# Two of four token chunks transposed by DMA ahead of use, rstd of the first tiles by Sqrt, and the last tile in halves

## The chip, the cores and the metric

The kernel runs on one core of a Trainium2 chip. A core has five engines with their own instruction queues, which run beside each other and wait for each other through semaphores: TensorE (PE in the profile, with PEld for its weight loads), VectorE (DVE), ScalarE (ACT), GpSimd (POOL) and SyncE (SP), which here only issues DMAs. The metric is the device time of one execution in microseconds, and what counts is the median over several executions.

## What is computed

x has 2048 tokens of 512 features, in bf16. The reference normalizes x and gives the result to two branches: an attention over a sliding window of 8 keys, 2 tokens apart, with 32 heads of 16 features, and a gated feed-forward block with 1792 hidden features. The output is x plus the product of the attention and the Silu of the feed-forward block.

```python
def _layernorm(x, axis=-1, eps=1e-5):
    m = jnp.mean(x, axis=axis, keepdims=True)
    v = jnp.var(x, axis=axis, keepdims=True)
    return (x - m) / jnp.sqrt(v + eps)
...
    def _A_ref(x, wqkv, wo):
        ...
        logits = jnp.einsum("bhsd,bhswd->bhsw", q, kg) * scale
        logits = jnp.where(mask[None, None, :, :], logits, -1e9)
        attn = _softmax(logits, axis=-1)
        o = jnp.einsum("bhsw,bhswd->bhsd", attn, vg)
        return (lambda x, *d: x.transpose(*d))(o, 0, 2, 1, 3).reshape(B, S, D) @ wo
    def _B_ref(x, w_gate, w_up, w_down):
        g = jnp.einsum("bsd,df->bsf", x, w_gate)
        u = jnp.einsum("bsd,df->bsf", x, w_up)
        h = _gelu(g) * u
        return jnp.einsum("bsf,fd->bsd", h, w_down)
    x = A_x
    xn = _layernorm(x, axis=-1)
    s = _A_ref(xn, A_wqkv, A_wo)
    g = _silu(_B_ref(xn, B_w_gate, B_w_up, B_w_down))
    return x + s * g
```

## The kernel before

The 2048 tokens are 16 tiles of 128 (t) and four chunks of 512 (j), four tiles each. For each chunk there are three stages, in which PE works nearly without a pause: qkv (12 groups of four matmuls that give q, k and v with features on the partitions), glu (14 groups: gate and up products, Gelu on ACT, their product h on DVE), and down (four tiles: the 14 matmuls of the down product y, the four of the attention's output product s, then Silu, product and sum). The order of stages is qkv of chunk 0, glu of chunk 0, qkv of chunk 1, down of chunk 0, glu of chunk 1, qkv of chunk 2, down of chunk 1, and so on: a chunk's qkv stage stands between the glu and the down stage of the chunk before.

Each engine runs its instructions in the order in which the program's text issues them; there is no scheduler. What belongs to another chunk is put between by a table: `at((stage, j, i), fn, ...)` hangs a step ahead of group i of a stage, and `run(stage, j, i)` issues what hangs there (lines 392 to 438 hold the table, 467 to the end the loops).

The steps that the change touches:

- `moments(t)` (line 169) takes mean and variance of a tile on DVE, adds epsilon on DVE, and takes the power -0.5 on GpSimd to get rstd. `normalize(t)` (line 179) makes xn on DVE, one of four buffers of the pool sm4.
- `transpose(t)` (line 186) makes four 128x128 transposes of xn on PE into one PSUM tile `tr`, which ACT copies into `xnT[j]` (features on partitions, the moving operand of all qkv and glu matmuls). xnT has two buffers, so chunk 2 takes chunk 0's and chunk 3 takes chunk 1's.
- The table puts chunk 1's transposes into the glu stage of chunk 0, and those of chunks 2 and 3 into the qkv stages of chunks 1 and 2:

```python
        at(("qkv", 1, 1 + 3 * i), transpose, 2 * TPQ + i)
        at(("qkv", 2, 3 + 2 * i), transpose, 3 * TPQ + i)
```

- `warm_up(n, cols)` (line 200) issues matmuls on zeros, so that PE isn't idle until the first data is there.
- `project` (line 208) is the group of four matmuls, one for each block of 128 input features. `qkv(j, fo, i0, n)` (line 220) is a group with its evacuation by ACT; for chunk 0 it runs over two halves of 256 tokens.
- `down(j, tt)` (line 357) treats the very last tile in two column halves from s onwards, with the second half's store issued by ACT; y and its Silu are whole.
- All PSUM tiles of `tr`, `qkv_ps`, `g_ps`, `u_ps`, `y_ps`, `s_ps`, `sp_ps` and the warm-up rotate through five buffers (pool mm).
- SyncE's queue holds, in this order: the loads of x and the weights; then for each chunk the stores of v to a DRAM scratch (`vT<-vst`, line 235, in the qkv stage), and in the down stage by turns a load of shifted v (`v_arr<-vT`, line 243) and a store of the output (line 387).

Of the kernel before, what the change touches and what calls it, by code (L numbers as in the profile page):

```python
# [9 lines left out]
AF = mybir.ActivationFunctionType  # L10
BF16 = mybir.dt.bfloat16
F32 = mybir.dt.float32

P = 128
# [7 lines left out]
TQ = 512  # L22
VW = TQ + WL * DIL
EPS = 1e-5
# [4 lines left out]
def kernel(  # L29
# [13 lines left out]
    nc = tc.nc  # L43
    B, S, D = A_x.shape
    DF = B_w_gate.shape[1]
    NT, NC, NF, NJ = S // P, D // P, DF // P, S // TQ
    TPQ = TQ // P
    SV = PAD + S
    x2d, out2d = A_x[0], out[0]
# [3 lines left out]
    def pool(name, bufs, **kw):  # L53
        return ctx.enter_context(tc.tile_pool(name=name, bufs=bufs, **kw))

    const = pool("const", 1)
# [7 lines left out]
    xtp = pool("xtp", 2)  # L64
# [5 lines left out]
    mm = pool("mm", 5, space=bass.MemoryType.PSUM)  # L70
# [3 lines left out]
    x_sb = big.tile([P, NT, D], BF16, name="x_sb")  # L74
    wqkv_sb = wts.tile([P, NC, 3 * D], BF16, name="wqkv_sb")
    wg_sb = wts.tile([P, NC, DF], BF16, name="wg_sb")
    wu_sb = wts.tile([P, NC, DF], BF16, name="wu_sb")
    wd_sb = wts.tile([P, NF, D], BF16, name="wd_sb")
# [24 lines left out]
    def load_late_weights():  # L103
# [7 lines left out]
            )  # L111


    warm = const.tile([P, TQ], BF16, name="warm")
    nc.vector.memset(warm[:], 0.0)
    ident = const.tile([P, P], BF16, name="ident")
    make_identity(nc, ident[:])
# [1 line left out]
        out=vT.rearrange("(k p) n -> p k n", p=P)[:, :, 0:PAD],  # L119
        in_=warm[:, 0 : NC * PAD].rearrange("p (k n) -> p k n", k=NC),  # L120
# [19 lines left out]
    def sum_constants():  # L140

        nc.gpsimd.memset(dsum[:], 0.0)
        for c in range(NC):
            nc.gpsimd.memset(dsum[:, c, 8 * c : 8 * c + 8], 1.0)
            band(dsum[:, c, 8 * c : 8 * c + 8], 0, 16, 16, 1, 8)
        for j in range(WL):
            nc.gpsimd.tensor_copy(
                out=hsum[H * j : H * (j + 1), :],
                in_=ident[H * j : H * (j + 1), H * j : H * (j + 1)],
            )  # L150
        nc.gpsimd.memset(spread[:], 0.0)
        for q in range(4):
            for j in range(4):
                nc.gpsimd.tensor_copy(
                    out=spread[H * q : H * (q + 1), q, H * j : H * (j + 1)],
                    in_=ident[H * q : H * (q + 1), H * q : H * (q + 1)],
                )

    xnT = {}
    k_sb = big.tile([P, NC, PAD + S], BF16, name="k_sb")  # L160
    nc.vector.memset(k_sb[:, :, 0:PAD], 0.0)
    stats = const.tile([P, NT, nc.vector.BN_STATS_DIM], F32, name="stats")
    mv = const.tile([P, NT, nc.vector.BN_AGGR_DIM], F32, name="mv")
    mhalf = const.tile([P, 1], F32, name="mhalf")
    nc.gpsimd.memset(mhalf[:], -0.5)
    rstd = const.tile([P, NT, 1], F32, name="rstd")


    def moments(t):
        nc.vector.bn_stats(out=stats[:, t, :], in_=x_sb[:, t, :])  # L170
        nc.vector.bn_aggr(out=mv[:, t, :], in_=stats[:, t, :])
        nc.vector.tensor_scalar(  # L172
            out=rstd[:, t, :], in0=mv[:, t, 1:2], scalar1=EPS, scalar2=None, op0=ALU.add
        )
        nc.gpsimd.tensor_tensor(out=rstd[:, t, :], in0=rstd[:, t, :], in1=mhalf[:], op=ALU.pow)  # L175

    xns = {}

    def normalize(t):
        xn = xns[t] = sm4.tile([P, D], BF16, name="xn")  # L180
        nc.vector.tensor_scalar(
            out=xn[:], in0=x_sb[:, t, :], scalar1=mv[:, t, 0:1], scalar2=rstd[:, t, :],
            op0=ALU.subtract, op1=ALU.mult,
        )

    def transpose(t):
        xn = xns[t]
        tr = mm.tile([P, NC * P], BF16, name="tr", tag="mm")
        for c in range(NC):
            nc.tensor.transpose(tr[:, c * P : (c + 1) * P], xn[:, c * P : (c + 1) * P], ident[:])  # L190
        j, i = divmod(t, TPQ)
        if i == 0:
            xnT[j] = xtp.tile([P, NC, TQ], BF16, name="xnT")
        nc.scalar.activation(  # L194
            out=xnT[j][:, :, i * P : (i + 1) * P],
            in_=tr[:].rearrange("p (c n) -> p c n", c=NC),
            func=AF.Copy,
        )

    def warm_up(n, cols):  # L200

        ps = mm.tile([P, TQ], F32, name="warm_ps", tag="mm")
        for _ in range(n):
            nc.tensor.matmul(
                ps[:, 0:cols], lhsT=warm[:, 0:P], rhs=warm[:, 0:cols], start=True, stop=True
            )

    def project(ps, w, lo, j, i0=0, n=TQ):
        for dk in range(NC):
            nc.tensor.matmul(  # L210
                ps[:],
                lhsT=w[:, dk, lo : lo + P],
                rhs=xnT[j][:, dk, i0 : i0 + n],
                start=(dk == 0),
                stop=(dk == NC - 1),
            )

    st = [dict(pk={}, pv={}) for _ in range(NJ)]

    def qkv(j, fo, i0=0, n=TQ):  # L220
        which, c = divmod(fo, NC)
        if fo == 0 and i0 == 0:
            st[j]["q"] = qp.tile([P, NC, TQ], BF16, name="q_sb")
        ps = mm.tile([P, n], F32, name="qkv_ps", tag="mm")
        project(ps, wqkv_sb, fo * P, j, i0, n)
        if which == 0:
            nc.scalar.activation(out=st[j]["q"][:, c, i0 : i0 + n], in_=ps[:], func=AF.Copy)  # L227
        elif which == 1:
            lo = PAD + j * TQ + i0
            nc.scalar.activation(out=k_sb[:, c, lo : lo + n], in_=ps[:], func=AF.Copy)  # L230
        else:
            vst = sm4.tile([P, TQ], BF16, name="vst")
            nc.scalar.activation(out=vst[:], in_=ps[:], func=AF.Copy)  # L233
            lo = PAD + j * TQ
            nc.sync.dma_start(out=vT[c * P : (c + 1) * P, lo : lo + TQ], in_=vst[:])
# [119 lines left out]
        st[j][fc] = h  # L355

    def down(j, tt):
        y = mm.tile([P, D], F32, name="y_ps", tag="mm")
        for fc in range(NF):
            nc.tensor.matmul(  # L360
                y[:],
                lhsT=st[j][fc][:, tt * P : (tt + 1) * P],
                rhs=wd_sb[:, fc, :],
                start=(fc == 0),
                stop=(fc == NF - 1),
            )
        sl = sm2.tile([P, D], BF16, name="sl")
        nc.scalar.activation(out=sl[:], in_=y[:], func=AF.Silu)  # L368
        t = j * TPQ + tt
        o_t = sm4.tile([P, D], BF16, name="o_t")  # L370
        pieces = 2 if t == NT - 1 else 1
        n = D // pieces
        for i in range(pieces):
            cols = slice(i * n, (i + 1) * n)
            s = mm.tile([P, n], F32, name="s_ps", tag="mm")
            for g in range(NC):
                nc.tensor.matmul(  # L377
                    s[:],
                    lhsT=st[j]["oT"][:, g, tt * P : (tt + 1) * P],
                    rhs=wo_sb[:, g, cols],  # L380
                    start=(g == 0),
                    stop=(g == NC - 1),
                )
            m = sm2.tile([P, n], BF16, name="m")
            nc.vector.tensor_tensor(out=m[:], in0=s[:], in1=sl[:, cols], op=ALU.mult)  # L385
            nc.vector.tensor_tensor(out=o_t[:, cols], in0=m[:], in1=x_sb[:, t, cols], op=ALU.add)
            (nc.scalar if i else nc.sync).dma_start(
                out=out2d[t * P : (t + 1) * P, cols], in_=o_t[:, cols]
            )


    side = {}
# [1 line left out]
    def at(key, fn, *args):  # L394
        side.setdefault(key, []).append((fn, args))
# [5 lines left out]
    for i in range(TPQ):  # L401
        at(("qkv", 0, i), normalize, TPQ + i)
        at(("glu", 0, 7 + i), moments, 2 * TPQ + i)
        at(("glu", 0, i), transpose, TPQ + i)
        at(("glu", 0, 8 + i), normalize, 2 * TPQ + i)
        at(("qkv", 1, 1 + 3 * i), transpose, 2 * TPQ + i)
        at(("glu", 1, 10 + i), moments, 3 * TPQ + i)
        at(("qkv", 2, 2 * i), normalize, 3 * TPQ + i)
        at(("qkv", 2, 3 + 2 * i), transpose, 3 * TPQ + i)

    for w in range(W):
        at(("glu", 0, w), qk_product, 0, w)
# [26 lines left out]


    HT = TPQ // 2
    warm_up(9, TQ)
    moments(0)
    moments(1)
    normalize(0)
    transpose(0)
    normalize(1)
    warm_up(2, P)
    transpose(1)
    warm_up(2, P)  # L450
    moments(2)
    moments(3)
    normalize(2)
    normalize(3)
    for t in range(TPQ, 2 * TPQ):
        moments(t)
    sum_constants()
    for hh in range(2):
        for fo in range(2 * NC):
            qkv(0, fo, hh * HT * P, HT * P)  # L460
            if hh == 0 and fo in (2, 4):
                transpose(HT + fo // 2 - 1)
    for i in range(NC):
        run("qkv", 0, i)
        run("qkv", 0, NC + i)
        qkv(0, 2 * NC + i)
# [41 lines left out]
```

The softmax here doesn't subtract the row's maximum and nothing guards it: scores larger than these inputs give would overflow.

## Time and profile before

| What | us |
|---|---|
| median of 8 runs | 234.62 |
| lowest and highest run | 234.46 and 234.8 |
| the profiled execution, its time | 234.71 |
| the profiled execution, its span | 233.0 |

The span is what the profiler shows of the program, from its first to its last instruction; 1.7 us of the execution's time lie around it. Where the time goes, by stage (PE busy in the stretch, and the engines' own stages don't overlap on PE):

| Stretch of the span, us | What runs on PE | Length | PE busy |
|---|---|---|---|
| 0 to 7.5 | warm-up, two tiles transposed | 7.51 | 5.10 |
| 7.5 to 18.6 | qkv of chunk 0 | 11.09 | 11.04 |
| 18.6 to 46.0 | glu of chunk 0, chunk 1 transposed | 27.40 | 27.24 |
| 46.0 to 59.2 | qkv of chunk 1, chunk 2 transposed, attention of chunk 0 | 13.20 | 13.10 |
| 59.2 to 74.8 | down of chunk 0 | 15.60 | 15.55 |
| 74.8 to 103.4 | glu of chunk 1, attention of chunk 1 | 28.60 | 28.28 |
| 103.4 to 114.7 | qkv of chunk 2, chunk 3 transposed | 11.30 | 11.25 |
| 159.0 to 169.4 | qkv of chunk 3 | 10.40 | 10.35 |
| 213.6 to 233.0 | down of chunk 3 and the end | 19.40 | 15.50 |

A line of a timeline reads: start in us, length in us, engine, line of the program, operation, what it writes and what it reads, shapes, how many in a row; in brackets the idle time of the engine ahead of it and what ended it. SPq is SyncE's queue issuing a DMA. Consecutive matmuls overlap in the records, so what one costs PE is the distance between starts.

### The profile page before, as it was taken

To read this page: it belongs to the slowest core of one execution; us is meant where nothing else is said; L and a number is where in the kernel's file an instruction comes from. 1 tells how busy PE (TensorE), PEld (TensorE's weight loads), DVE (VectorE), ACT (ScalarE), POOL (GpSimd) and SP (SyncE) were. 2 spreads that over 40 slices of the span, in tenths; PEclk is the share of its full clock that TensorE was granted. 3 is DMA by queue.
4 is the path that set the end of the run, shared out by engine and by line. 5 is a ranking of instruction groups with operands and counts; after the bars stand their busy time and mean duration, and the time that the engine had idled before them with its cause. 6 is when DMAs were issued, how large, how long until landed. Compare 5 with 4: busy or idle time off the path is not lost.

```text
span 233.0 us, 3499 instructions
## 1 busy us (share of the span) xinstructions
PE 225.2 (97%) x1321; PEld 105.5 (45%) x1345; DVE 146.4 (63%) x232; ACT 135.6 (58%) x222; POOL 24.5 (11%) x64
## 2 busy tenths in 40 slices
PE   7899999999999999999999999999999999999993
PEld 2775444444444444445444444444444444444441
DVE  4583996996795198981669139951349429864132
ACT  2779869777513865758821396657641387576211
POOL 3248943100000000130000000000000000000000
PEclk9999999999999999999999999999999999999999
DMA  5999399921288200000257600000047910000001
GB/s 156 362 373 366 102 203 203 286 81 48 70 184 200 50 0 0 3 0 0 82 140 177 153 1 3 0 0 3 23 126 169 199 32 0 0 3 1 23 23 45
DMA packets 21937, 22.66 MB, mean 97 GB/s; under 512 B 1568, under 2 KB 21920, under 8 KB 21920
## 3 DMA queue, kind: packets, MB, share of 16 engines
q1 hardware_dynamic: 21776, 22.37, 36.3%
q8 instruction: 10, 0.16, 0.3%
q10 hardware_dynamic: 144, 0.07, 0.1%
q14 instruction: 7, 0.06, 0.1%
HBM read 18.22 MB, written 4.21 MB: 96 GB/s over the span
## 4 chain that ended last, share of the span: by engine, by line
PE 93%; DMA 2%; ACT 1%; issue 1%; SPq 1%; DVE 1%; ACTq 0%
PE u_ps L210 21%; PE y_ps L360 21%; PE g_ps L210 20%; PE qkv_ps L210 18%; PE s_ps L377 6%; PE o_ps L325 3%; PE L_ps L265 3%; DMA wqkv_sb<-in_A_wqkv_dram 2%; PE tr L190 1%; ACT u L352 1%; SPq L83 1%; PE den_ps L285 0%; PE sp_ps L300 0%; DVE m L385 0%; ACT sl L368 0%
## 5 line engine op out<-in xcount | busy, mean ns | idle before, releaser
L210 PE MATMUL u_ps<-xnT,wu_sb 128*128 128x512 bf16 x221 | 57.0, 379 | 0.2
L210 PE MATMUL g_ps<-xnT,wg_sb 128*128 128x512 bf16 x212 | 55.9, 379 | 0.8 <-issue 0.5
L360 PE MATMUL y_ps<-wd_sb,h 128*128 128x512 bf16 x220 | 50.6, 379 | 0.2
L255 DVE TENSOR_TENSOR pk<-q_sb,k_sb 128x2048 bf16<-128x2048 bf16 x32 | 37.8, 1219 | 12.2 <-ACT k_sb L230 12.2
L354 DVE TENSOR_TENSOR h<-ge,u 128x512 bf16<-128x512 bf16 x56 | 23.7, 424 | 34.1 <-ACT u L352 33.9
L210 PE MATMUL qkv_ps<-xnT,wqkv_sb 128*128 128x512 bf16 (+1 forms) x219 | 43.9, 348 | 1.0 <-DMA wqkv_sb<-in_A_wqkv_dram 0.8
L350 ACT ACTIVATE ge<-g_ps 128x512 bf16<-128x512 f32 x56 | 33.6, 601 | 14.4 <-PE g_ps L210 12.3
L352 ACT ACTIVATE u<-u_ps 128x512 bf16<-128x512 f32 x56 | 33.6, 600 | 13.9 <-PE u_ps L210 13.9
L311 DVE TENSOR_TENSOR pv<-E,v_arr 128x2048 bf16<-128x2048 bf16 x32 | 38.6, 1216 | 0.0
L368 ACT ACTIVATE sl<-y_ps 128x512 bf16<-128x512 f32 x16 | 9.6, 597 | 43.9 <-PE y_ps L360 40.6
L210 PEld LDWEIGHTS <-wu_sb 128*128 128x128 bf16 x224 | 21.9, 98 | 26.6 <-issue 0.3
L360 PEld LDWEIGHTS <-h 128*128 128x128 bf16 x224 | 21.9, 98 | 26.4
L210 PEld LDWEIGHTS <-wg_sb 128*128 128x128 bf16 x224 | 20.8, 98 | 26.7 <-issue 4.2
L210 PEld LDWEIGHTS <-wqkv_sb 128*128 128x128 bf16 x224 | 21.3, 98 | 18.6 <-DMA wqkv_sb<-in_A_wqkv_dram 1.0
L385 DVE TENSOR_TENSOR m<-s_ps,sl 128x512 bf16<-128x512 f32 (+1 forms) x17 | 11.2, 656 | 26.8 <-PE s_ps L377 24.4
L175 POOL TENSOR_TENSOR rstd<-rstd,mhalf 128x1 f32<-128x1 f32 x16 | 10.4, 653 | 78.1 <-DVE rstd L172 78.1
L377 PE MATMUL s_ps<-wo_sb,oT 128*128 128x512 bf16 (+1 forms) x68 | 16.4, 367 | 0.1
L170 DVE BATCH_NORM_STATS2 stats<-x_sb 128x6 f32<-128x512 bf16 x16 | 11.0, 686 | 4.3 <-DMA x_sb<-in_A_x_dram 4.3
L227 ACT ACTIVATE q_sb<-qkv_ps 128x512 bf16<-128x512 f32 (+1 forms) x20 | 10.2, 512 | 4.9 <-PE qkv_ps L210 4.6
L233 ACT ACTIVATE vst<-qkv_ps 128x512 bf16<-128x512 f32 x16 | 9.6, 597 | 5.0 <-PE qkv_ps L210 5.0
L194 ACT ACTIVATE xnT<-tr 128x512 bf16<-128x512 bf16 x16 | 9.5, 597 | 4.0 <-PE tr L190 4.0
L230 ACT ACTIVATE k_sb<-qkv_ps 128x512 bf16<-128x512 f32 (+1 forms) x20 | 10.2, 512 | 2.1 <-PE qkv_ps L210 1.9
(42 smaller groups left out, 121.5 us busy)
## 6 DMA issues: line engine op xcount, KB each, us to landing
v_arr<-vT SPq DMA_DIRECT2D x16, 520.0 KB, 5.1
vT<-vst SPq DMA_DIRECT2D x16, 128.0 KB, 1.7
out_dram<-o_t SPq DMA_DIRECT2D x15, 128.0 KB, 2.6
wg_sb<-in_B_w_gate_dram SPq DMA_DIRECT2D x2, 896.0 KB
wu_sb<-in_B_w_up_dram SPq DMA_DIRECT2D x2, 896.0 KB, 13.2
wd_sb<-in_B_w_down_dram SPq DMA_DIRECT2D x1, 1792.0 KB, 17.2
wqkv_sb<-in_A_wqkv_dram SPq DMA_DIRECT2D x3, 512.0 KB, 5.8
x_sb<-in_A_x_dram SPq DMA_DIRECT2D x3, 512.0 KB, 10.1
```

Of the source, the lines that this page charges most:

```text
L170: nc.vector.bn_stats(out=stats[:, t, :], in_=x_sb[:, t, :])
L175: nc.gpsimd.tensor_tensor(out=rstd[:, t, :], in0=rstd[:, t, :], in1=mhalf[:], op=ALU.pow)
L210: nc.tensor.matmul(ps[:], lhsT=w[:, dk, lo : lo + P], rhs=xnT[j][:, dk, i0 : i0 + n], start=(dk == 0), stop=(dk == NC - 1),)
L227: nc.scalar.activation(out=st[j]["q"][:, c, i0 : i0 + n], in_=ps[:], func=AF.Copy)
L255: nc.vector.tensor_tensor(out=pk[:], in0=st[j]["q"][:], in1=k_sb[:, :, off : off + TQ], op=ALU.mult)
L311: nc.vector.tensor_tensor(out=pv[:], in0=st[j]["E"][:, wh, :].unsqueeze(1).to_broadcast([P, 4, TQ]), in1=st[j]["va"][:, 4 * g : 4 * g + 4, ...
L350: nc.scalar.activation(out=ge[:], in_=g_ps[:], func=AF.Gelu_apprx_tanh)
L352: nc.scalar.activation(out=u[:], in_=u_ps[:], func=AF.Copy)
L354: nc.vector.tensor_tensor(out=h[:], in0=ge[:], in1=u[:], op=ALU.mult)
L360: nc.tensor.matmul(y[:], lhsT=st[j][fc][:, tt * P : (tt + 1) * P], rhs=wd_sb[:, fc, :], start=(fc == 0), stop=(fc == NF - 1),)
L377: nc.tensor.matmul(s[:], lhsT=st[j]["oT"][:, g, tt * P : (tt + 1) * P], rhs=wo_sb[:, g, cols], start=(g == 0), stop=(g == NC - 1),)
L385: nc.vector.tensor_tensor(out=m[:], in0=s[:], in1=sl[:, cols], op=ALU.mult)
```

## The change

Six things, in the order of the program's text:

1. The warm-up tile has 256 columns instead of 512, with 17 matmuls of 256 columns instead of 9 of 512, and runs of four instead of two small ones between the first transposes.
2. For the first four tiles rstd is computed as the reciprocal (DVE) of Sqrt(variance + epsilon) (ACT). A Sqrt over a constant at the start brings that function's table in ahead of the data. The other twelve tiles keep the power on GpSimd.
3. Chunk 0's first half of tokens: the four q groups are multiplied feature block pair by feature block pair (blocks 0 and 1 of all four, then 2 and 3), tile 1's copy is in two pieces, and the tiles 2 and 3 are transposed after the q groups, with their copies on DVE. The moments of chunk 1 come after that.
4. The tiles of chunks 2 and 3 are transposed by DMA: 16 requests of 128x128 for a chunk, on SyncE's queue, issued at the head of the glu stages of chunks 1 and 2. Their PE transposes and ACT copies are gone.
5. `project` and `qkv` get arguments for item 3.
6. In `down` the last tile's y and Silu are also made in two halves, each followed by its own s, product, sum and store, both stores on SyncE.

```diff
--- before.py
+++ after.py
@@ -111,7 +111,7 @@
             )
 
 
-    warm = const.tile([P, TQ], BF16, name="warm")
+    warm = const.tile([P, TQ // 2], BF16, name="warm")
     nc.vector.memset(warm[:], 0.0)
     ident = const.tile([P, P], BF16, name="ident")
     make_identity(nc, ident[:])
@@ -166,6 +166,23 @@
     rstd = const.tile([P, NT, 1], F32, name="rstd")
 
 
+    epsc = const.tile([P, 1], F32, name="epsc")
+    nc.gpsimd.memset(epsc[:], EPS)
+    std = const.tile([P, TPQ, 1], F32, name="std")
+
+    nc.scalar.activation(out=std[:, 0, :], in_=epsc[:], func=AF.Sqrt, bias=epsc[:], scale=1.0)
+
+    def first_moments(t):
+        nc.vector.bn_stats(out=stats[:, t, :], in_=x_sb[:, t, :])
+        nc.vector.bn_aggr(out=mv[:, t, :], in_=stats[:, t, :])
+        nc.scalar.activation(
+            out=std[:, t, :], in_=mv[:, t, 1:2], func=AF.Sqrt, bias=epsc[:], scale=1.0
+        )
+
+    def first_normalize(t):
+        nc.vector.reciprocal(out=rstd[:, t, :], in_=std[:, t, :])
+        normalize(t)
+
     def moments(t):
         nc.vector.bn_stats(out=stats[:, t, :], in_=x_sb[:, t, :])
         nc.vector.bn_aggr(out=mv[:, t, :], in_=stats[:, t, :])
@@ -183,7 +200,7 @@
             op0=ALU.subtract, op1=ALU.mult,
         )
 
-    def transpose(t):
+    def transpose(t, parts=1, copy=None):
         xn = xns[t]
         tr = mm.tile([P, NC * P], BF16, name="tr", tag="mm")
         for c in range(NC):
@@ -191,11 +208,14 @@
         j, i = divmod(t, TPQ)
         if i == 0:
             xnT[j] = xtp.tile([P, NC, TQ], BF16, name="xnT")
-        nc.scalar.activation(
-            out=xnT[j][:, :, i * P : (i + 1) * P],
-            in_=tr[:].rearrange("p (c n) -> p c n", c=NC),
-            func=AF.Copy,
-        )
+        dst = xnT[j][:, :, i * P : (i + 1) * P]
+        src = tr[:].rearrange("p (c n) -> p c n", c=NC)
+        for k in range(parts):
+            c = slice(k * NC // parts, (k + 1) * NC // parts)
+            if copy is None:
+                nc.scalar.activation(out=dst[:, c], in_=src[:, c], func=AF.Copy)
+            else:
+                copy(out=dst[:, c], in_=src[:, c])
 
     def warm_up(n, cols):
 
@@ -205,8 +225,19 @@
                 ps[:, 0:cols], lhsT=warm[:, 0:P], rhs=warm[:, 0:cols], start=True, stop=True
             )
 
-    def project(ps, w, lo, j, i0=0, n=TQ):
-        for dk in range(NC):
+    def transpose_by_dma(t):
+        j, i = divmod(t, TPQ)
+        if i == 0:
+            xnT[j] = xtp.tile([P, NC, TQ], BF16, name="xnT")
+        for c in range(NC):
+            nc.sync.dma_start(
+                out=xnT[j][:, c, i * P : (i + 1) * P],
+                in_=xns[t][:, c * P : (c + 1) * P],
+                transpose=True,
+            )
+
+    def project(ps, w, lo, j, i0=0, n=TQ, dks=range(NC)):
+        for dk in dks:
             nc.tensor.matmul(
                 ps[:],
                 lhsT=w[:, dk, lo : lo + P],
@@ -217,12 +248,13 @@
 
     st = [dict(pk={}, pv={}) for _ in range(NJ)]
 
-    def qkv(j, fo, i0=0, n=TQ):
+    def qkv(j, fo, i0=0, n=TQ, ps=None):
         which, c = divmod(fo, NC)
         if fo == 0 and i0 == 0:
             st[j]["q"] = qp.tile([P, NC, TQ], BF16, name="q_sb")
-        ps = mm.tile([P, n], F32, name="qkv_ps", tag="mm")
-        project(ps, wqkv_sb, fo * P, j, i0, n)
+        if ps is None:
+            ps = mm.tile([P, n], F32, name="qkv_ps", tag="mm")
+            project(ps, wqkv_sb, fo * P, j, i0, n)
         if which == 0:
             nc.scalar.activation(out=st[j]["q"][:, c, i0 : i0 + n], in_=ps[:], func=AF.Copy)
         elif which == 1:
@@ -355,23 +387,22 @@
         st[j][fc] = h
 
     def down(j, tt):
-        y = mm.tile([P, D], F32, name="y_ps", tag="mm")
-        for fc in range(NF):
-            nc.tensor.matmul(
-                y[:],
-                lhsT=st[j][fc][:, tt * P : (tt + 1) * P],
-                rhs=wd_sb[:, fc, :],
-                start=(fc == 0),
-                stop=(fc == NF - 1),
-            )
+        t = j * TPQ + tt
+        halves = [slice(0, D // 2), slice(D // 2, D)] if t == NT - 1 else [slice(0, D)]
+        n = D // len(halves)
         sl = sm2.tile([P, D], BF16, name="sl")
-        nc.scalar.activation(out=sl[:], in_=y[:], func=AF.Silu)
-        t = j * TPQ + tt
         o_t = sm4.tile([P, D], BF16, name="o_t")
-        pieces = 2 if t == NT - 1 else 1
-        n = D // pieces
-        for i in range(pieces):
-            cols = slice(i * n, (i + 1) * n)
+        for i, cols in enumerate(halves):
+            y = mm.tile([P, n], F32, name="y_ps", tag="mm")
+            for fc in range(NF):
+                nc.tensor.matmul(
+                    y[:],
+                    lhsT=st[j][fc][:, tt * P : (tt + 1) * P],
+                    rhs=wd_sb[:, fc, cols],
+                    start=(fc == 0),
+                    stop=(fc == NF - 1),
+                )
+            nc.scalar.activation(out=sl[:, cols], in_=y[:], func=AF.Silu)
             s = mm.tile([P, n], F32, name="s_ps", tag="mm")
             for g in range(NC):
                 nc.tensor.matmul(
@@ -384,9 +415,7 @@
             m = sm2.tile([P, n], BF16, name="m")
             nc.vector.tensor_tensor(out=m[:], in0=s[:], in1=sl[:, cols], op=ALU.mult)
             nc.vector.tensor_tensor(out=o_t[:, cols], in0=m[:], in1=x_sb[:, t, cols], op=ALU.add)
-            (nc.scalar if i else nc.sync).dma_start(
-                out=out2d[t * P : (t + 1) * P, cols], in_=o_t[:, cols]
-            )
+            nc.sync.dma_start(out=out2d[t * P : (t + 1) * P, cols], in_=o_t[:, cols])
 
 
     side = {}
@@ -403,10 +432,10 @@
         at(("glu", 0, 7 + i), moments, 2 * TPQ + i)
         at(("glu", 0, i), transpose, TPQ + i)
         at(("glu", 0, 8 + i), normalize, 2 * TPQ + i)
-        at(("qkv", 1, 1 + 3 * i), transpose, 2 * TPQ + i)
+        at(("glu", 1, 0), transpose_by_dma, 2 * TPQ + i)
         at(("glu", 1, 10 + i), moments, 3 * TPQ + i)
         at(("qkv", 2, 2 * i), normalize, 3 * TPQ + i)
-        at(("qkv", 2, 3 + 2 * i), transpose, 3 * TPQ + i)
+        at(("glu", 2, 0), transpose_by_dma, 3 * TPQ + i)
 
     for w in range(W):
         at(("glu", 0, w), qk_product, 0, w)
@@ -439,27 +468,37 @@
 
 
     HT = TPQ // 2
-    warm_up(9, TQ)
-    moments(0)
-    moments(1)
-    normalize(0)
+    HQ = HT * P
+    warm_up(17, TQ // 2)
+    first_moments(0)
+    first_moments(1)
+    first_normalize(0)
     transpose(0)
-    normalize(1)
-    warm_up(2, P)
-    transpose(1)
-    warm_up(2, P)
-    moments(2)
-    moments(3)
-    normalize(2)
-    normalize(3)
+    first_normalize(1)
+    warm_up(4, P)
+    transpose(1, parts=2)
+    warm_up(4, P)
+    first_moments(2)
+    first_moments(3)
+    first_normalize(2)
+    first_normalize(3)
+
+    qs = [mm.tile([P, HQ], F32, name="qkv_ps", tag="mm") for _ in range(NC)]
+    for dks in ((0, 1), (2, 3)):
+        for fo in range(NC):
+            project(qs[fo], wqkv_sb, fo * P, 0, 0, HQ, dks)
+    for fo in range(NC):
+        qkv(0, fo, 0, HQ, qs[fo])
+    transpose(HT, copy=nc.vector.tensor_copy)
+    for fo in range(NC, 2 * NC):
+        qkv(0, fo, 0, HQ)
+        if fo == NC:
+            transpose(HT + 1, copy=nc.vector.tensor_copy)
     for t in range(TPQ, 2 * TPQ):
         moments(t)
     sum_constants()
-    for hh in range(2):
-        for fo in range(2 * NC):
-            qkv(0, fo, hh * HT * P, HT * P)
-            if hh == 0 and fo in (2, 4):
-                transpose(HT + fo // 2 - 1)
+    for fo in range(2 * NC):
+        qkv(0, fo, HQ, HQ)
     for i in range(NC):
         run("qkv", 0, i)
         run("qkv", 0, NC + i)
```

## Prediction

> **What bounds the kernel now.** I read the page's busy shares first, then the chain of work that ended last, then the timeline of the tensor engine where the change touches it, and SyncE's own timeline, because the change gives SyncE new work.
>
> ```profile
> PE 225.2 (97%) x1321; PEld 105.5 (45%) x1345; DVE 146.4 (63%) x232; ACT 135.6 (58%) x222; POOL 24.5 (11%) x64
> PE 93%; DMA 2%; ACT 1%; issue 1%; SPq 1%; DVE 1%; ACTq 0%
> ```
>
> PE is busy for 97% of the span and carries 93% of the chain. So an edit pays only where it takes work off PE, or where PE stands still now: the start, and the last microseconds. The start, from the chain in order of time:
>
> ```profile
> 2.66 4.81 DMA wqkv_sb<-in_A_wqkv_dram
> 7.46 0.05 issue
> 7.51 1.48 PE qkv_ps L210 x12
> ```
>
> The first real matmul waits for the first third of wqkv, landed at 7.46. The stage table by windows has PE busy 11.04 of the 11.09 us from there to the first glu stage: no hole to win. One qkv stage, from the PE timeline (start, us, instruction, count):
>
> ```profile
> 103.34 2.75 PE L210 MATMUL qkv_ps<-xnT,wqkv_sb 128*128 128x512 bf16 x12
> 105.93 0.39 PE L190 MATMUL tr<-ident,xn 128*128 128x128 bf16 x4
> 106.15 1.89 PE L210 MATMUL qkv_ps<-xnT,wqkv_sb 128*128 128x512 bf16 x8
> ```
>
> The busy time of matmuls overlaps, so the price of a tile's transpose is from start to start: 106.15 - 105.93 = 0.22 us, not the 0.39 shown. SyncE's timeline between the store that ends a down stage and the first store of the next qkv stage:
>
> ```profile
> 76.16 0.33 SPq L387 DMA_DIRECT2D out_dram<-o_t  x1
> 112.60 3.13 SPq L235 DMA_DIRECT2D vT<-vst  x4
> ...
> 131.58 0.33 SPq L387 DMA_DIRECT2D out_dram<-o_t  x1
> 167.51 2.91 SPq L235 DMA_DIRECT2D vT<-vst  x4
> ```
>
> SyncE issues nothing in the glu stages of chunks 1 and 2, and the stage table has the DMA engines 8% busy there. The end, from the timeline of all engines:
>
> ```profile
> 228.12 1.04 PE L377 MATMUL s_ps<-wo_sb,oT 128*128 128x256 bf16 x8
> 228.32 0.60 ACT L368 ACTIVATE sl<-y_ps 128x512 bf16<-128x512 f32 x1 [3.29 <-PE y_ps L360]
> 228.95 0.42 DVE L385 TENSOR_TENSOR m<-s_ps,sl 128x256 bf16<-128x256 f32 x1 [2.43 <-ACT sl L368]
> 229.41 0.29 DVE L386 TENSOR_TENSOR o_t<-m,x_sb 128x256 bf16<-128x256 bf16 x1
> 229.62 0.42 DVE L385 TENSOR_TENSOR m<-s_ps,sl 128x256 bf16<-128x256 f32 x1
> ```
>
> Both halves of the last tile wait for one Silu over 512 columns, then go through DVE one after the other.
>
> **What the Trainium skill says.** "VectorE: DVE Perf Modes", section on the three transpose paths, puts a 128x128 bf16 transpose at 390 ns on TensorE and 1309 ns through the DMA crossbar. The trace has 0.22 us of PE time for four in a pipeline, so the first figure is a lone latency; no run here shows the second. "DMA: Bandwidth & Descriptors", in its rules for kernel authors, says that a transpose next to ordinary DMAs needs nothing; untested here. "ScalarE: Activation LUTs", section on what ACT_TABLE_LOAD costs, gives 1283 ns whatever the set; the trace's loads are all 1283 ns. "TensorE: Matmul & The Clock Gate", part 1, says that the array runs at half clock until it was busy for a window of about 3.4 us that doesn't start with the kernel. The trace agrees in kind: warm-up matmuls of 512 columns start 0.43 us apart, later ones 0.22.
>
> **The change part by part.**
>
> Transposes of chunks 2 and 3. Removed: 8 tiles of 4 PE transposes, 8 x 0.22 = 1.76 us, all on the path, since PE is without a hole in both qkv stages; and 8 ACT evacuations of 0.6 us, beside PE. Not all of it comes through. In chunk 1's qkv stage the spread matmuls (sp_ps, line 300) wait for the reciprocals:
>
> ```profile
> 50.06 0.95 DVE L294 RECIPROCAL rs<-den_ps 128x128 bf16<-128x128 f32 x1
> ```
>
> That ends at 51.01, behind a DVE queue with no gap since 43.66, so it doesn't move. sp_ps starts at 51.38 now; two removed tiles (at 46.28 and 50.29) bring it to 50.94, where it must wait until about 51.07 (0.06 us from DVE's end to PE, as at the first transpose, 5.30 to 5.36). I deduct 0.13. What else is near doesn't bite: the last attention product ends at 54.35 and its sums move from 56.46 to about 55.7; in chunk 2's qkv stage DVE idles 5.80 us before its products.
>
> Added: 16 DMA transposes of 128x128 for each of the two chunks, in SyncE's queue behind the store above. The order of the built program has nothing else between that store and the v stores of the next stage, so they start at 76.16 + 0.33 = 76.5 and 131.9. Each has a semaphore of eight in rotation, so it waits for the one eight places earlier. PE wants the first rows of the new xnT at 103.34 and the sixteenth piece (last column block) three matmuls of 0.22 later, 104.0; for chunk 3, 159.08 + 0.65 = 159.7. Stages ahead of it shorten both sides alike. The cost c of one is unseen. From below: 0.33 us, what the store of 128 rows takes to issue. From above: no overlap at all, issue plus landing of a v store, 0.33 + 1.7 = 2.03 us (the page's median to landing is 1.7). I take the skill's 1.309: 16 x 1.309 = 20.9, plus 1.7 for the last to land, 76.5 + 22.6 = 99.1, and 154.5. That is 4.9 and 5.2 us ahead of need. So PE never waits: cost nothing, hidden by the glu stage. It stays so up to c = (104.0 - 76.5 - 1.7) / 16 = 1.61 us. Queued behind a late one would be the next stage's v stores, not due before 112.6.
>
> What reads and frees buffers: the normalize of chunk 3 (in chunk 2's qkv stage) overwrites xn after the DMAs read it, which PE needed first anyway. The two xnT buffers were last read by the glu stage before. Nothing new waits there.
>
> rstd by Sqrt, splitting, order of the start. An Add and a Power on GpSimd (0.55 us and a hop) give way to a Sqrt on ACT and a reciprocal of one column on DVE. The Sqrt isn't in the trace; near 0.3 us, below the 0.38 of a 256-column ACTIVATE; the reciprocal near the 0.15 of the one-column Add. Tile 0's xn starts at about 4.95 (4.89 before), since DVE does tile 1's moments first; tile 1's goes from 5.75 to about 5.5. Both are done well before 7.46, when the weights land, and those are requested in the same place: gain 0. The table load is one for one, at 0.80, under the loads of x. Behind 7.51 PE does the same multiplications and two transposes in another order. The third transpose now comes at 7.51 + 16 x 0.109 = 9.25, and its xn is there at 8.5 even by the old path; the two copies moved to DVE (0.6 us each) end near 10.9, and the second half of the columns starts at 11.4. So 0 again, with bounds of -0.2 and +0.3, five PSUM buffers in rotation being the reason for the upper one.
>
> The end. The last tile's down product in two halves: 28 matmuls of 0.109 for 14 of 0.216, the same 3.0 us. Half 0's Silu, product and store run under half 1's matmuls. Then y of half 1 ends its issue at 225.10 + 1.52 + 0.44 + 1.53 = 228.59; Silu 0.2 later, 0.38 long, to 229.17; s ends at 229.03, and 0.27 later (as for the tile before) DVE may start: 229.30. Product 0.42 and addition 0.29 with their small gaps end at 230.04, against 230.35 now. The last store is issued by SyncE and not by ACT, 0.33 for 0.38. Gain 0.31; bounds 0.1 to 0.45.
>
> Sum: 1.76 - 0.13 + 0 + 0.31 = 1.94 us. The profiled execution took 234.71 (span 233.0 and 1.7 around it), so 232.8 for its like; it lies 0.09 above the median of 234.62, so 232.7 for a median. Own range of this case 232.0 to 233.4.
>
> **The rivals.**
>
> Transposes late (slower). One mechanism: SyncE or the crossbar takes more than 1.61 us for each, and PE stands at the head of the qkv stages of chunks 2 and 3. With the upper price, 2.03, the last lands at 76.5 + 32.5 = 109.0 and 164.4: 5.0 + 4.7 = 9.7 us late, less 1.94: 234.62 + 7.8 = 242.4. For it: the trace shows no such DMA, they are small, 32 KB, and there are 16 of them in one queue. Against it: 4.9 us to spare at the page's figure, an empty queue and idle DMA engines.
>
> Half the gain. Removing transposes brings PE up against DVE and PSUM evacuation at more places than sp_ps, for instance the attention sums in chunk 1's qkv stage, and chunk 1's 0.9 us is lost: 233.6. For it: DVE is busy 11.13 of 13.2 us in that stage. Against: each later dependence has 0.7 us or more in hand.
>
> Cold start. The warm-up now has 17 x 256 columns for 9 x 512, ends 0.25 us earlier, and PE idles longer before the first xn. If the clock is still halved at 7.51, up to 3.4 us run at half speed: 1.7 us lost, total 234.4, no change. Against: the two runs of extra small warm-up matmuls, and 3.6 us of unbroken work.
>
> **How the numbers follow.** Forecast 0.66, half the gain 0.06, cold start 0.04, late 0.24. A change below 0.2% (0.47 us) can't be told from none here. Faster: forecast and half the gain, less a rest, 0.71. Same: 0.05. Slower: 0.24. The three cases other than late lie between 232.0 and 234.5 and hold 0.76, so the range must take in the milder half of late: up to 242.5. It is 232.0 to 242.5.
>
> **What would show it.** Right: no tr in the two qkv stages; those stages 0.75 and 0.9 us shorter; PE's qkv_ps not waiting for a DMA of xnT; the last transpose landed before 104 less what came earlier; the last o_t about 0.3 us closer to the last y_ps; the first qkv_ps still near 7.5, released by wqkv_sb. Wrong: DMA xnT as what PE waits for, at 1.6 us or more for each request; matmuls 0.2 us apart at 256 columns after 7.5; a new idle row before s_ps or o_ps.

## Result and profile after

The changed kernel takes 232.72 us in the median of 11 runs (232.41 to 233.23), against 234.61 for the kernel before in the same comparison. The ratio is 0.9916, 95% interval 0.9906 to 0.9925: faster by 0.84%. Of the kernel before, 1 execution of 32 here took 236.28 us, and 3 or 4 of 27 beside each later group of runs took 236.15 to 236.79 at a mean granted clock of 0.989 to 0.993, which widens the intervals and hardly moves the medians. The profiled execution took 232.77 with a span of 231.1, against 234.71 and 233.0. The page of the changed kernel begins as follows, with the busy shares and further down the chain by engine:

```profile
PE 223.6 (97%) x1315; PEld 106.5 (46%) x1339; DVE 147.0 (64%) x234; ACT 132.2 (57%) x219; POOL 22.1 (10%) x61
...
PE 91%; DVE 4%; ACT 2%; DMA 1%; issue 1%; ACTq 0%; DVEq 0%
```

PE lost 1.6 us of busy time and still fills 97% of the span. But DVE's share of the chain went from 1% to 4%: somewhere the kernel now waits for DVE. SyncE's timeline of the changed kernel, at the ends of the down stages of chunks 0 and 1:

```profile
75.47 0.33 SPq L418 DMA_DIRECT2D out_dram<-o_t  x1
75.91 21.89 SPq L233 DMA_TRANSPOSE xnT<-xn  x16
...
130.00 0.33 SPq L418 DMA_DIRECT2D out_dram<-o_t  x1
130.43 20.73 SPq L233 DMA_TRANSPOSE xnT<-xn  x16
```

16 requests take 21.9 and 20.7 us, 1.37 and 1.30 each. The trace gives 2.3 us in the median from a request to its landing, so the last of chunk 2, requested near 75.91 + 21.89 - 1.23 = 96.6, lands near 98.9. PE wants it near 103.3. The next stage of the kernel before, then this stretch of the changed one:

```profile
114.59 1.67 PE L360 MATMUL y_ps<-wd_sb,h 128*128 128x512 bf16 x7
```

```profile
101.78 1.03 PE L241 MATMUL u_ps<-xnT,wu_sb 128*128 128x512 bf16 x4
102.65 10.52 PE L241 MATMUL qkv_ps<-xnT,wqkv_sb 128*128 128x512 bf16 x47
113.01 3.18 PE L398 MATMUL y_ps<-wd_sb,h 128*128 128x512 bf16 x14
```

The stage runs from 102.65 to 113.01 in one piece, 10.36 us against 11.25 (103.34 to 114.59), and no line of PE's waits names xnT. Chunk 1's qkv stage shows where DVE comes in; PE's timeline before, then after:

```profile
48.45 1.04 PE L325 MATMUL o_ps<-pv,hsum 128*32 128x512 bf16 x16
```

```profile
47.98 0.82 PE L357 MATMUL o_ps<-pv,hsum 128*32 128x512 bf16 x12
49.07 0.40 PE L357 MATMUL o_ps<-pv,hsum 128*32 128x512 bf16 x4 [0.27 <-DVE pv L343]
49.40 1.90 PE L241 MATMUL qkv_ps<-xnT,wqkv_sb 128*128 128x512 bf16 x7
51.14 0.39 PE L332 MATMUL sp_ps<-rs,spread 128*128 128x128 bf16 x4
```

The first attention sums, which ran in one piece before (48.45 to 49.42), now stop after 12 of 16 matmuls, until DVE has the fourth product pv. The view names 0.27 us of idle time; from the first sum to the next qkv matmul it is 1.42 us instead of 0.97. PE begins the stage 0.25 us earlier, but DVE's products stand where they stood. DVE's timeline before, then after:

```profile
42.99 0.41 DVE L181 TENSOR_SCALAR xn<-x_sb,mv,rstd 128x512 bf16<-128x512 bf16 x1 [0.44 <-POOL rstd L175]
46.65 3.49 DVE L311 TENSOR_TENSOR pv<-E,v_arr 128x2048 bf16<-128x2048 bf16 x3
```

```profile
43.06 0.41 DVE L198 TENSOR_SCALAR xn<-x_sb,mv,rstd 128x512 bf16<-128x512 bf16 x1 [0.76 <-POOL rstd L192]
46.66 3.48 DVE L343 TENSOR_TENSOR pv<-E,v_arr 128x2048 bf16<-128x2048 bf16 x3
50.07 0.95 DVE L326 RECIPROCAL rs<-den_ps 128x128 bf16<-128x128 f32 x1
```

Counted from the start of the stage, the third product begins at 1.49 us instead of 1.23. DVE lost this ahead of them: to normalize the last tile of chunk 2 it now waits 0.76 us for GpSimd instead of 0.44. The run start_only, below, shows which part of the change does that.

The end, from the timeline of all engines, before and after:

```profile
230.06 0.29 DVE L386 TENSOR_TENSOR o_t<-m,x_sb 128x256 bf16<-128x256 bf16 x1
```

```profile
227.20 0.38 ACT L405 ACTIVATE sl<-y_ps 128x256 bf16<-128x256 f32 x1 [1.58 <-PE y_ps L398]
227.71 0.43 DVE L416 TENSOR_TENSOR m<-s_ps,sl 128x256 bf16<-128x256 f32 x1 [1.22 <-PE s_ps L408]
228.17 0.29 DVE L417 TENSOR_TENSOR o_t<-m,x_sb 128x256 bf16<-128x256 bf16 x1
```

Only one half's Silu, product and sum now stand behind the last matmuls. Subtracting the starts of the same instruction in both traces gives the account:

| Mark | before | after | so far | by this stretch |
|---|---|---|---|---|
| first qkv matmul | 7.51 | 7.26 | -0.25 | -0.25 |
| qkv of chunk 1 begins | 45.42 | 45.17 | -0.25 | 0 |
| down of chunk 0 begins | 59.18 | 58.49 | -0.69 | -0.44 |
| qkv of chunk 2 begins | 103.34 | 102.65 | -0.69 | 0 |
| down of chunk 1 begins | 114.59 | 113.01 | -1.58 | -0.89 |
| last o_t ends | 230.35 | 228.46 | -1.89 | -0.31 |

### The profile page after: what moved, and what is told of

The parts are those of the page before. It is cut to its first block, busy times and chain, and to the rows that moved or that the text cites. A ratio compares the mean times of both kernels' runs of the same rounds, so it can differ in the third digit from the quotient of the medians.

```text
span 231.1 us, 3521 instructions
## 1 busy us (share of the span) xinstructions
PE 223.6 (97%) x1315; PEld 106.5 (46%) x1339; DVE 147.0 (64%) x234; ACT 132.2 (57%) x219; POOL 22.1 (10%) x61
## 4 chain that ended last, share of the span: by engine, by line
PE 91%; DVE 4%; ACT 2%; DMA 1%; issue 1%; ACTq 0%; DVEq 0%
PE y_ps L398 21%; PE u_ps L241 20%; PE g_ps L241 20%; PE qkv_ps L241 17%; PE s_ps L408 6%; PE L_ps L297 3%; PE o_ps L357 3%; DVE pv L343 2%; DMA x_sb<-in_A_x_dram 1%; PE tr L207 1%; ACT u L384 1%; DVE stats L176 1%; ACT xnT L216 0%; DVE h L386 0%; PE sp_ps L332 0%
## 5 line engine op out<-in xcount | busy, mean ns | idle before, releaser
L398 PE MATMUL y_ps<-wd_sb,h 128*128 128x512 bf16 (+1 forms) x234 | 50.9, 366 | 0.2
L241 PE MATMUL qkv_ps<-xnT,wqkv_sb 128*128 128x512 bf16 (+1 forms) x219 | 42.8, 348 | 1.0 <-ACT std L178 0.7
L398 PEld LDWEIGHTS <-h 128*128 128x128 bf16 x238 | 23.3, 98 | 25.3
L405 ACT ACTIVATE sl<-y_ps 128x512 bf16<-128x512 f32 (+1 forms) x17 | 9.7, 572 | 44.0 <-PE y_ps L398 44.0
L241 PEld LDWEIGHTS <-wu_sb 128*128 128x128 bf16 x224 | 21.9, 98 | 26.6 <-issue 0.3
L192 POOL TENSOR_TENSOR rstd<-rstd,mhalf 128x1 f32<-128x1 f32 x12 | 8.0, 665 | 79.8 <-DVE rstd L189 77.6
L369 DVE TENSOR_TENSOR oT<-o_ps,rb 128x1024 bf16<-128x1024 f32 x8 | 9.7, 1217 | 1.4 <-PE o_ps L357 1.4
L408 PEld LDWEIGHTS <-oT 128*128 128x128 bf16 x68 | 6.7, 98 | 7.2
```

What stands on the lines that cost most here:

```text
L241: nc.tensor.matmul(ps[:], lhsT=w[:, dk, lo : lo + P], rhs=xnT[j][:, dk, i0 : i0 + n], start=(dk == 0), stop=(dk == NC - 1),)
L369: nc.vector.tensor_tensor(out=st[j]["oT"][:, 2 * gg : 2 * gg + 2, :], in0=st[j]["o"][:], in1=st[j]["rb"][:].unsqueeze(1).to_broadcast([P, ...
L398: nc.tensor.matmul(y[:], lhsT=st[j][fc][:, tt * P : (tt + 1) * P], rhs=wd_sb[:, fc, cols], start=(fc == 0), stop=(fc == NF - 1),)
L408: nc.tensor.matmul(s[:], lhsT=st[j]["oT"][:, g, tt * P : (tt + 1) * P], rhs=wo_sb[:, g, cols], start=(g == 0), stop=(g == NC - 1),)
```

## Experiments

The theory after this reading: the gain is PE time freed in two qkv stages, plus the end; in chunk 1's stage part of it is eaten by DVE. The rivals: start and end carry the gain; the pieces simply add up; or the DMA transposes are near their limit. Each was timed beside the kernel before, whose medians there were 234.64 to 234.67.

### The change in parts

**pe_back**: the changed kernel with the two lines of the table put back.

```diff
-        at(("glu", 1, 0), transpose_by_dma, 2 * TPQ + i)
+        at(("qkv", 1, 1 + 3 * i), transpose, 2 * TPQ + i)
-        at(("glu", 2, 0), transpose_by_dma, 3 * TPQ + i)
+        at(("qkv", 2, 3 + 2 * i), transpose, 3 * TPQ + i)
```

> The changed kernel with the transposes of chunks 2 and 3 back on PE, at the old places; start and end as changed. Theory (the gain is PE time freed by the DMA transposes, 1.3 of the 1.9 us, and the end 0.3): 234.1 to 234.4 us, so 0.2 to 0.5 below before. Rival (start and end carry the gain, and the transposes were hidden anyway): 233.6 or less.

Measured: 234.33, ratio 0.999 (0.9972 to 1.0008). That is within the theory's range. Without the DMA transposes 0.31 us are left, what the account gives the end.

**dma_only**: the kernel before with the opposite two lines and the new function, nothing else.

> The kernel before with nothing but the DMA transposes of chunks 2 and 3. Theory (in chunk 1's qkv stage PE runs into the fourth attention product of DVE, which eats what PE has gained up to there; the start's 0.25 us and one transpose share that one hole): o_ps waits about 0.1 us instead of 0.27, the stage is about 0.7 us shorter than before, chunk 3's 0.9, together 233.0. Rival (each part's gain in the trace stands by itself, 0.44 and 0.89): 233.3.

Measured: 232.96, ratio 0.9921 (0.9901 to 0.9942). PE's timeline of dma_only:

```profile
45.29 2.75 PE L221 MATMUL qkv_ps<-xnT,wqkv_sb 128*128 128x512 bf16 x12
...
48.09 1.23 PE L336 MATMUL o_ps<-pv,hsum 128*32 128x512 bf16 x16
...
58.34 1.89 PE L371 MATMUL y_ps<-wd_sb,h 128*128 128x512 bf16 x8
```

The theory's numbers came true. The stage lasts 58.34 - 45.29 = 13.05 us against 13.76 before: 0.71 won, where the whole change won 0.44. The 16 sums take 1.23 us instead of 1.04, a hole of 0.19: with one transpose less ahead of them, PE runs into the fourth product. The theory's reason for the larger loss in the full change, that an earlier start is paid back in this hole, is not what the next traces show.

**end_only**: the kernel before with the new `down`. **start_only**: the kernel before with items 1, 2, 3 and 5 of the change.

> The kernel before with nothing but the last tile's y and Silu in halves and both stores on SyncE. Theory (the end is worth what the trace shows, 0.3 us, whatever else is changed): 234.3. Rival (the end's gain is only a shift in the records, since the last store lands when it did): 234.6, no change.

> The kernel before with nothing but the start: warm-up, rstd of four tiles by Sqrt, split q groups, two copies on DVE. Theory (the first qkv matmul waits for the later of xnT's copies and the first third of wqkv; the change brings the copies forward from 7.3 to about 6.9, so that the weights' landing decides, and that varies by some tenths from run to run): 234.3 to 234.6, with more spread than before, first qkv matmul between 6.9 and 7.5. Rival (the earlier start seen in the trace is a gain of 0.25 us in each run): 234.35 with the spread of before.

Measured: end_only 234.18 (ratio 0.9984, 0.9958 to 1.0009), start_only 234.73 (0.9996, 0.998 to 1.0012). In end_only's trace the last o_t ends at 229.93, 0.42 earlier, of which 0.11 are its start (7.40 for 7.51): 0.31 from the end, as in the change. The median moved by 0.47. The interval includes no change, but 11 of the 14 runs (234.07 to 234.38) lie below all 27 of the kernel before (234.44 and more); how much the end is worth, the trace says. start_only gained nothing, and both its time and its first matmul fell outside what the theory had expected. That matmul, from PE's timeline:

```profile
7.72 1.48 PE L241 MATMUL qkv_ps<-xnT,wqkv_sb 128*128 128x256 bf16 x12 [1.22 <-DMA wqkv_sb<-in_A_wqkv_dram]
```

xnT's copies were done at 7.02 there, and PE waited for the weights till 7.7. The same start gave 7.26 in the change, 6.97 in pe_back and 7.20 in all_dma below, where the weights are the last to come or close to it. So the 0.25 us of the account are the landing of one DMA in one execution.

The new start also costs time, further on. GpSimd's power and DVE's normalize for the last tile of chunk 2, in the kernel before and then in start_only, where the first attention sums follow:

```profile
42.37 0.59 POOL L175 TENSOR_TENSOR rstd<-rstd,mhalf 128x1 f32<-128x1 f32 x1 [1.85 <-DVE rstd L172]
```

```profile
42.92 0.55 POOL L192 TENSOR_TENSOR rstd<-rstd,mhalf 128x1 f32<-128x1 f32 x1 [2.18 <-DVE h L386]
43.50 0.41 DVE L198 TENSOR_SCALAR xn<-x_sb,mv,rstd 128x512 bf16<-128x512 bf16 x1 [0.73 <-POOL rstd L192]
48.66 1.25 PE L357 MATMUL o_ps<-pv,hsum 128*32 128x512 bf16 x16
```

GpSimd used to begin as soon as DVE had added epsilon. In start_only it begins after the instruction that follows in DVE's queue, a product h, and DVE waits 0.73 us for it instead of 0.44. So the third product pv begins 1.47 us into chunk 1's qkv stage instead of 1.23, and the stage, all its transposes still on PE, lasts 13.97 us instead of 13.76. pe_back has the same (1.47 and 13.96). All traces with the new start in which PE transposes chunk 1 have it at 1.46 to 1.49, and all four with the old start (before, dma_only, end_only, before_swap) at 1.23. Why GpSimd's instruction now waits for h, no view names.

An earlier first matmul, on the other hand, is kept: in the change, two_more, six_more, one_request and change_swap it comes between 6.90 and 7.26, and the stage lasts 13.29 to 13.32 us in each. So the new start takes 0.2 us from this stage, whenever PE starts.

The parts' medians, -1.68, -0.47 and +0.08, add up to -2.07 against -1.9 measured, so the pieces add up within what the runs can tell. dma_only and end_only alone make -2.15; the change without its new start wasn't built.

### How far ahead the transposes are

**two_more** and **six_more**: 2 or 6 requests into a scratch tile ahead of each chunk's 16. The edit of six_more:

```diff
+    junk = const.tile([P, 6, P], BF16, name="junk")
     def transpose_by_dma(t):
...
+        for e in range(6 if i == 0 else 0):
+            nc.sync.dma_start(
+                out=junk[:, e, :], in_=xns[t][:, 0:P], transpose=True
+            )
```

> The changed kernel with 2 additional DMA transposes in front of each chunk's 16, into a scratch tile that nothing reads. Theory (one costs SyncE some 1.35 us, one after the other, and the last lands some 3 us ahead of need): they fit, 232.7 as the change, PE waits for no DMA. Rival (the cushion is smaller than the trace makes it look, because PE's wait needs all eight semaphores): 1 us or more above the change.

> The same with 6 additional requests. Theory: the last lands near 75.9 + 22 x 1.35 + 2.3 = 107.9, 4.6 us late, and for chunk 3 about 3.5 us late: 240 to 241.5, with PE's first qkv matmuls of both stages waiting for DMA xnT. Rival (the requests overlap, and their spacing in the trace is only a matter of the semaphores): under 234.

Measured: two_more 232.68 (0.9908, 0.9883 to 0.9934), six_more 240.51 (1.0213, 1.0168 to 1.0258). Both times are where the theories put them. The limit lies between 18 and 22 requests, as the spacing of 1.3 to 1.4 us says. PE's waits and timeline of six_more:

```profile
PE qkv_ps L247 <- DMA xnT<-xn: 5.2, 7, 1.2
```

```profile
102.98 0.39 PE L247 MATMUL qkv_ps<-xnT,wqkv_sb 128*128 128x512 bf16 x1 [0.27 <-DMA xnT<-xn]
104.52 0.38 PE L247 MATMUL qkv_ps<-xnT,wqkv_sb 128*128 128x512 bf16 x1 [1.15 <-DMA xnT<-xn]
105.77 0.39 PE L247 MATMUL qkv_ps<-xnT,wqkv_sb 128*128 128x512 bf16 x1 [0.87 <-DMA xnT<-xn]
107.02 11.57 PE L247 MATMUL qkv_ps<-xnT,wqkv_sb 128*128 128x512 bf16 x45 [0.87 <-DMA xnT<-xn]
```

Each of the first four matmuls needs the last tile's next column block, so they come at the pace of the requests. The fourth was due near 103.2 (the last u_ps group ends its issue at 101.69 + 0.86, and three matmuls of 0.22 follow) and comes at 107.02, 3.8 us late; for chunk 3 it is 165.91 for 163.4, 2.5 late. That is 6.3, but the span grew by 8.2 over two_more's. The rest stands in the windows table of six_more for these matmuls (length, PE busy, PEld busy, then granted clock):

```profile
107.00:108.00 1.00, 0.98 (x4) 0.47 (x5) 0.74 0.00 0
108.00:109.00 1.00, 1.00 (x4) 0.31 (x3) 0.50 0.00 0
109.00:110.00 1.00, 1.00 (x4) 0.31 (x3) 0.50 0.00 0
110.00:111.00 1.00, 1.00 (x4) 0.42 (x3) 0.55 0.00 0
111.00:112.00 1.00, 1.00 (x7) 0.43 (x5) 1.00 0.00 0
```

After 4.3 us in which PE did three matmuls (102.72 to 107.02), its clock was granted at 0.50 for some 3.4 us, and half of that is lost: 1.7 more. This fits the Trainium skill ("TensorE: Matmul & The Clock Gate", part 1), which has the array back at half clock after an idle window of about 3.4 us; here the stretch was not wholly idle. Chunk 3's shorter gap (2.8 us with two matmuls) shows no such drop. The four timed runs bear the loss out: one kept a mean clock of 1.0 and took 238.39, the other three, at 0.99, took 240.34 to 240.72. That the gap causes the drop is what the trace suggests; no run tests it, and some executions of the kernel before have such a mean clock without this gap. So six_more's time agrees with its theory partly by luck: the waits are 0.8 and 1.0 us shorter than the 4.6 and 3.5 expected, and the clock makes up for them.

**one_request**: one DMA transpose for a tile.

```diff
-        for c in range(NC):
-            nc.sync.dma_start(
-                out=xnT[j][:, c, i * P : (i + 1) * P],
-                in_=xns[t][:, c * P : (c + 1) * P],
-                transpose=True,
-            )
+        nc.sync.dma_start(
+            out=xnT[j][:, :, i * P : (i + 1) * P], in_=xns[t][:], transpose=True
+        )
```

> The changed kernel with one DMA transpose for a whole tile of 128x512 instead of four of 128x128. Time as the change under either theory, 232.7, as long as the work is ahead of need. If the cost is SyncE's for each request, four requests take some 5.5 us for a chunk; if it is for the data, 128 columns at a time, they take some 21 us as before.

Measured: 232.62 (0.9899, 0.9866 to 0.9932), no different from the change. What a request takes (ns, lowest, median, highest), from the view of the tile xnT, first of the changed kernel and then of one_request:

```profile
L233 SPq DMA_TRANSPOSE xnT<-xn x32: 1136/1230/2015, 75.9 to 149.9; - x32
```

```profile
L232 SPq DMA_TRANSPOSE xnT<-xn x8: 1247/1262/1874, 75.8 to 134.2; - x8
```

1.26 us for 128x512 as for 128x128: the cost is SyncE's for the request, the same for 512 columns as for 128. A chunk takes 5.8 us of the queue instead of 21.9.

### Making use of it

**sums_later**: the change with the sums one group later.

```diff
-    at(("qkv", 1, 3), av_sums, 0, 0)
+    at(("qkv", 1, 4), av_sums, 0, 0)
-    at(("qkv", 1, 5), spread_reciprocals, 0)
+    at(("qkv", 1, 6), spread_reciprocals, 0)
```

> The changed kernel with the first attention sums of chunk 0 one group later (group 4 of chunk 1's qkv stage instead of 3) and the spread one group later. Theory (the 0.27 us in which o_ps waits for the product pv is PE time lost): the wait goes, 232.4 to 232.5. Rival (what is won there is lost at the next thing that waits for DVE, the spread or the second sums): 232.7.

Measured: 232.33 (0.9887, 0.9857 to 0.9916), 0.39 below the change, with an interval that overlaps its. PE's timeline:

```profile
48.20 1.04 PE L241 MATMUL qkv_ps<-xnT,wqkv_sb 128*128 128x512 bf16 x4
49.16 1.05 PE L357 MATMUL o_ps<-pv,hsum 128*32 128x512 bf16 x16
50.14 1.90 PE L241 MATMUL qkv_ps<-xnT,wqkv_sb 128*128 128x512 bf16 x7
```

The sums run in one piece again. The stage lasts 13.10 us (45.28 to 58.38), 0.22 less than in the change.

**all_dma**: sums_later with one request for a tile, and chunk 1's four tiles by DMA too.

```diff
-        at(("glu", 0, i), transpose, TPQ + i)
...
+    for t in range(TPQ, 2 * TPQ):
+        transpose_by_dma(t)
     load_v(0)
```

> The kernel of sums_later, with one DMA transpose for a whole tile, and chunk 1's four tiles transposed by DMA too, requested behind chunk 0's v stores. Theory (four requests cost SyncE 5.3 us, so they fit into its wait for the v stores, and 4 x 0.22 us of PE time go from chunk 0's glu stage): 231.3 to 231.6. Rival (the requests push back the v loads, and DVE's first products of v come late): 232.3 or more, with pv waiting for DMA v_arr.

Measured: 232.11 (0.9885, 0.9864 to 0.9906); a miss. PE reaches chunk 1's qkv stage at 44.22, 1.06 earlier than in sums_later (0.17 of it the first matmul's), and leaves it at 58.10, 0.28 earlier. The chain of all_dma in that stretch (start, us, what):

```profile
43.55 1.23 DVE pv L340
44.78 0.34 DVE h L383
45.12 1.13 DVE pv L340
46.25 0.33 DVE h L383
46.58 3.41 DVE pv L340 x3
49.99 0.87 DVE rs L323
50.86 3.34 DVE pv L340 x3
54.20 1.15 DVE oT L366
55.34 0.04 issue
55.38 1.05 PE o_ps L354 x16
```

The whole stage is DVE's: products, reciprocals and division without a gap, and PE's second sums wait for the division, 0.57 us. Why the first product begins only at 43.55 stays open: the view names a matmul of g_ps, which that product doesn't read. The v loads were requested 1.7 us later than in the change (28.71 for 27.05); the last of the four, requested near 30.9, would land near 43.5 with the longest time of the view, 12.6 us. That fits the rival, but it was not tried apart.

**all_swap**, **change_swap**, **before_swap**: the first third of wqkv requested ahead of tiles 2 and 3 of x, in all_dma, the change and the kernel before.

```diff
     for t in range(TPQ):
         load_x(t)
-    for i in range(3):
+        if t == 1:
+            load_w(wqkv_sb, A_wqkv, 0, D)
+    for i in range(1, 3):
```

> all_dma with the first third of wqkv requested ahead of the tiles 2 and 3 of x. Theory (the start hangs on the landing of these weights, and behind it on xnT's copies near 6.9 us): first qkv matmul at 6.9, 0.2 to 0.5 us below all_dma. Rival (tiles 2 and 3 of x come late, and the third transpose waits for their normalize): no gain or a loss.

> The changed kernel with the same swap of loads. Theory (the change's early copies are worth something only if the weights are there): first qkv matmul at 6.9 in each run, 0.1 to 0.4 us below the change, 232.3 to 232.6, with less spread. Rival: 232.7.

> The kernel before with the same swap. Theory (its copies end at 7.25, so the weights can come earlier for little): first qkv matmul at 7.3, 0.1 to 0.2 us below before, 234.4 to 234.5. Rival (the weights alone set the start, in both kernels alike): the same gain as in change_swap.

Measured: all_swap 232.04 (0.9882, 0.9862 to 0.9901), change_swap 232.73 (0.9921, 0.9898 to 0.9945), before_swap 234.94 (1.0006, 0.9991 to 1.0021). The starts moved to 6.61 in all_swap (from 7.20), 7.09 in change_swap (from 7.26) and 7.43 in before_swap (from 7.51), each released by xnT's copies or right behind them. The times did not move beyond what the runs can tell. The theory had expected 0.1 to 0.5; the rival of change_swap, no gain, came true, and before_swap's median even lies above before's. The profiled executions do keep an earlier start: all_swap's is 0.59 us ahead of all_dma's at the first matmul, 0.51 at the end of chunk 1's qkv stage and 0.6 in the span (230.1 for 230.7). But all_dma's was the slowest of its six executions and all_swap's the second fastest, so this pair shows more than the medians do. When the weights landed in executions that were not profiled isn't on record. all_swap and all_dma are the fastest kernels here, 0.6 to 0.7 us below the change, and can't be told from each other.

## Why the prediction was right

232.7 was predicted and 232.72 measured. The likeliest case held, and its mechanism with it; that it met the number to 0.02 us is luck, since two errors of 0.25 and 0.3 us cancelled in the profiled execution.

- Bound by PE, no hole in the qkv stages: right. pe_back and dma_only put the gain in the transposes.
- A tile at 0.22 us of PE time: right. Chunk 3's stage won 0.89 = 4 x 0.22.
- Transposes hidden, at the Trainium skill's 1.309 us each ("VectorE: DVE Perf Modes", the three transpose paths) and landing at 99.1: right. The trace agrees, with 1.23 us in the median and a spacing of 1.37, and the last one landed near 98.9. To take the figure of one transpose as the spacing of requests was an assumption, and it came out; that it is the price of a request and not of its data, one_request showed.
- The deduction of 0.13 for sp_ps in chunk 1's stage: wrong place and size. sp_ps didn't wait. The step looked at the last product of the second sums (54.35) and passed over the fourth product of the first sums, which DVE finishes near 49.0, just when those sums need it. With the transposes alone (dma_only) the hole there is 0.19 and the stage wins 0.71, close to the 0.75 of the sum. The whole change wins 0.44, because its new start brings DVE's products 0.25 later, a cost that the prediction didn't have; sums_later moved the sums behind them, and the wait went.
- The start at 0: start_only, at 234.73, bears the number out, and that the weights and not rstd decide when PE starts was right; the profiled -0.25 was their landing. But the zero is in part luck: what an early landing gives is kept, and the new start takes 0.2 back in chunk 1's qkv stage. The prediction's upper bound of 0.3 covers that, but for another reason, the PSUM buffers.
- The end at 0.31: 0.31 in the account and in end_only's trace.
- Half the gain, the rival: its mechanism, PE running into DVE at the first attention sums, is there, at 0.19 us in dma_only instead of 0.9. What spoke against it, 0.7 us in hand at each later dependence, was wrong for these sums.
- Late, the rival: its mechanism is real, and six_more has it. Its point, 1.61 us for a request, fits with 18 requests hidden and 22 not. Its price left out the clock, which in six_more's trace is halved behind the long wait: 1.7 of 8.2 us.
- Cold start: not seen in the change; all 12 of its executions have a mean clock of 0.998 or more. The transposes in the start of the changed kernel are followed by 256-column matmuls 0.11 us apart (16 from 7.26 to 9.02).

## What to carry to other kernels

On a kernel that is bound by one engine, a step moved off that engine is worth its start-to-start distance there, but only up to the next instruction that waits for an engine whose own queue has not moved; list all such waits of the stage, the first of a group as well as the last. A DMA transpose can stand in for a tensor-engine transpose if its queue is empty for a stage ahead; count requests, not bytes: one for 512 columns held the queue for 1.26 us, one for 128 for 1.23. Time a part of a change by itself, and read its trace beyond the stretch that it edits: the rearranged start lost 0.2 us some 40 us further on, through an engine that is busy for a tenth of the span.

## What was not expected of the hardware

A DMA transpose of 128x128 and one of 128x512 (bf16, within SBUF) held SyncE's queue for 1.23 and 1.26 us, while an ordinary store of 128 rows held it for 0.33. After 4.3 us with three matmuls PE ran at half clock for about 3.4 us. The landing of the same weight load, requested at the same time, let the first matmul start anywhere from 6.97 to 7.72 us.
